# Retention and feed-forward on one core: w1 and w2 loaded by six converting GpSimd transfers, and the order ahead of the fifth step redone

## The chip, the cores and the metric

One Trainium2 chip, one of its cores. The metric is the time of one execution on the device in microseconds (us); the kernel before was run three times, with a median of 176.36 us (176.16 to 177.26). A kernel is compared with the kernel before on the same chip.

## The reference

Four sequences of 768 tokens with 8 heads of 64 go through a retention recurrence, and its output through a feed-forward product. Inputs and output are fp32.

```python
state = gamma[h] * state + outer(k[t], v[t])       # per batch and head
y[t]  = (1 / sqrt(64)) * (q[t] @ state)
x     = y, laid out as 3072 tokens x 512
a, b  = x @ w1, x @ w2                             # 512 -> 1024 each
out   = ((a * b) @ w3) @ w_out                     # 1024 -> 1024 -> 512
```

## The kernel before

The 3072 tokens are cut into 12 steps of 256 (T), three steps for each sequence; "step n" below is one of them. For each step the kernel turns q and k on TensorE (`turn`, L341; the result is copied from PSUM by `turned`), multiplies them into scores (`scores`, L377), masks those on VectorE (`mask`, L397), forms k'v (`kv`, L433), advances the state (`state`), and adds the part from the state (`inter`, L499) to the part from the scores (`av`, L525) in two PSUM banks. `x_out` scales the sum into the fp16 tile `xt`, which is the x of the step. The products x@w1 and x@w2 follow, a multiplied by b gives `ht`, and a product with W3O (L627, L639) gives the rows of the output. W3O is w3 @ w_out, made once at the start: w3 is converted, turned in 128 x 128 blocks, and multiplied with w_out by `w3_mm` (L276), four 256-column matmuls in a call; `w3_out` takes a finished block row out of PSUM.

Steps 0 and 1 use w1 and w2 as they are: `rows(W, n, uh, d)` (L604) is four matmuls of 256 columns with row block d of W (128 of the 512 rows), for half uh of the 1024 columns, and `rows_out` takes each finished bank out, a plain copy for w1 (`pa`) and the multiplication a*b for w2 (`ht`). From step 2 on the products are made with fewer multiplications by sums of weights (`combine`, `sums`, `prod`, L752); that part is a loop from step 3 on and is not touched.

All order is written out by hand: each engine executes its instructions in the order in which the program lists them, and waits where data or a buffer is missing. PSUM is eight banks, each with one name (K, S0, S1, X0, X1, F0, F1, F2) and one buffer; a tile in a bank can be filled only when the last reader of the bank's previous content is done. Names in rows of a trace leave the digit out (psF is F0, F1 or F2).

Inputs come by `fetch`, in the order of the list at the end of the program: every load is 512 KB and is issued on SyncE's queue (SP) into one of 18 fp32 stage tiles `st`. q, k and v come in runs of 512 bytes (128 floats, L85), weights in rows of 4096 bytes (L98, L103). k, q and the weights are then converted to fp16 by a copy on an engine ("s" ScalarE = ACT, "v" VectorE = DVE, "g" GpSimd = POOL; all by line 62), v is multiplied by a decay on POOL (`cast_v`, L65). w1 and w2 are eight such loads between v1 and k2, and 16 conversions: row blocks 0 and 2 in halves of 512 columns (`cast_wc`), blocks 1 and 3 in halves of 64 partitions that change places (`cast_wh`). `fence(n)` is a copy of one column on ACT (L510) that waits for the first half of `inter`.

```python
W1 = [wpool.tile([128, DFF], HP, name=f"w1_{i}") for i in range(4)]
def cast_wh(W, st, d, r, eng):
    copy(eng, W[d][half(1 - r), :], w_st[st, d][half(r), :])
```

Of the kernel before, what the change touches and what calls it, by code (L numbers as in the profile page):

```python
# [21 lines left out]
def kernel(  # L22
# [11 lines left out]
    nc = tc.nc  # L34
# [40 lines left out]
    tok_in = {}  # L75
    source = {"q": q, "k": k, "v": v}

    def load(nm, n, via=None):
        via = via or nc.sync
        b, c = divmod(n, PER)  # L80
        t = new_stage()
# [105 lines left out]
    W1 = [wpool.tile([128, DFF], HP, name=f"w1_{i}") for i in range(4)]  # L187
    W2 = [wpool.tile([128, DFF], HP, name=f"w2_{i}") for i in range(4)]
# [74 lines left out]
    W3_BANK = {4: 'K', 1: 'S0', 2: 'X0', 5: 'F2', 3: 'F0', 6: 'X1', 7: 'F2', 0: 'F2'}  # L263
# [326 lines left out]
    ROW_BANKS = {('a', 0, 0): ('F2', 'X0'), ('a', 0, 1): ('K', 'F1'), ('b', 0, 0): ('S0', 'X0'), ('b', 0, 1): ('X1', 'F1'), ('a', 1, 0): ('S1', 'F0'), ('a', 1, 1): ('K', 'F2'), ('b', 1, 0): ('S1', 'S0'), ('b', 1, 1): ('K', 'F1')}  # L590
# [92 lines left out]
    def cast_w(W, st, d, eng):  # L683
        copy(eng, W[d][:, :], w_st[st, d][:, :])

    def cast_wc(W, st, d, x, eng):
        copy(eng, W[d][:, x * 512 : x * 512 + 512], w_st[st, d][:, x * 512 : x * 512 + 512])

    def cast_wh(W, st, d, r, eng):
        copy(eng, W[d][half(1 - r), :], w_st[st, d][half(r), :])  # L690
# [150 lines left out]
    fetch("k0")  # L841
    fetch("r7")
    fetch("wo3")
# [3 lines left out]
    fetch("r0")  # L847
    fetch("k1")
    fetch("v1")
    fetch("w11")  # L850
    fetch("w10")
    fetch("w13")
    fetch("w12")
    fetch("w21")
    fetch("w22")
    fetch("w20")
    fetch("w23")
    fetch("k2")
# [56 lines left out]
    tables()  # L915
    w3_mm(3, 2)
    w3_mm(4, 1)
    w3_mm(1, 2)
    w3_mm(6, 2)
    w3_mm(3, 1)  # L920
    turn("k", 0, "F1")
    w3_mm(2, 1)
# [4 lines left out]
    w3_mm(3, 3)  # L927
# [4 lines left out]
    w3_mm(2, 3)  # L932
    w3_mm(6, 1)
    w3_mm(3, 0)
    w3_mm(7, 2)
    turned("k", 0, "v")
    w3_out(5, "v")
    turned("q", 0, "v")
    w3_out(1, "v")
    w3_out(4, "s")  # L940
    cast_v(0, "g")
    cast("q", 1, "s")
    scores(0, ("K", "F1"), 0)
    scores(0, ("S0", "S1"), 1)
# [3 lines left out]
    w3_mm(6, 0)  # L948
    w3_mm(7, 3)
# [3 lines left out]
    step_decays()  # L953
    w3_out(3, "v")
    mask(0, 0, 0)
    mask(0, 1, 1)
    mask(0, 1, 0)
    state(0, 1)
    mask(0, 0, 1)
# [3 lines left out]
    turn("q", 1, "F1")  # L963
    turn_w3(0, "S0")
    w3_out(2, "s")
    fence(0)
    state(0, 3)
    turned_w3(0, "v")
    inter(0, 1)
    av(0)  # L970
    cast("k", 1, "s")
    turned("q", 1, "v")
    cast_wh(W1, "w1", 1, 0, "s")
    turn("k", 1, "X0")
    cast_v(1, "g")
    turned("k", 1, "v")
    x_out(0, 0)
    x_out(0, 1)
    w3_mm(0, 2)
    w3_mm(0, 0)  # L980
    scores(1, ("S0", "X0"), 1)
    cast_wh(W1, "w1", 1, 1, "g")
    mask(1, 1, 1)
    w3_mm(0, 1)
# [4 lines left out]
    cast_wc(W1, "w1", 0, 0, "g")  # L989
    cast_wh(W1, "w1", 3, 0, "g")  # L990
    cast_wc(W1, "w1", 2, 1, "g")
    cast_wc(W1, "w1", 2, 0, "g")
    w3_out(0, "s")
    cast_wc(W1, "w1", 0, 1, "s")
    cast_wh(W1, "w1", 3, 1, "s")
    mask(1, 1, 0)
# [3 lines left out]
    rows(W1, 0, 0, 0)  # L1000
    rows(W1, 0, 1, 1)
    inter(1, 0, ("S0", "S1"))
    rows(W1, 0, 1, 3)
    rows(W1, 0, 0, 3)
    rows(W1, 0, 1, 2)
    fence(1)
    mask(1, 0, 0)
    state(1, 2)
    rows_out("a", 0, 1, 0, "s")
    cast_wh(W2, "w2", 1, 0, "v")  # L1010
    cast_wh(W2, "w2", 1, 1, "v")
    cast_wc(W2, "w2", 2, 1, "g")
# [5 lines left out]
    cast_wc(W2, "w2", 2, 0, "s")  # L1018
    cast_wh(W2, "w2", 3, 1, "s")
    x_out(1, 0)  # L1020
    rows(W2, 0, 1, 2)
    rows(W2, 0, 1, 1)
    rows(W2, 0, 0, 1)
    rows_out("a", 0, 0, 0, "v")
    x_out(1, 1)
    state(1, 3)
    cast_wc(W2, "w2", 0, 0, "g")
    cast_wc(W2, "w2", 0, 1, "g")
    cast_wh(W2, "w2", 3, 0, "g")
    combine(3, 0)  # L1030
    combine(1, 1)
    combine(3, 1)
    cast_v(2, "g")
    rows(W2, 0, 0, 0)
    rows(W2, 0, 1, 0)
    rows(W1, 1, 0, 3)
    rows(W1, 1, 0, 0)
    rows(W1, 1, 1, 1)
    rows(W1, 1, 0, 2)
    rows(W2, 0, 0, 2)  # L1040
    rows(W2, 0, 0, 3)
    rows(W1, 1, 0, 1)
    rows(W1, 1, 1, 0)
    rows(W1, 1, 1, 2)
    rows(W1, 1, 1, 3)
    rows(W2, 1, 0, 2)
    rows(W2, 0, 1, 3)
    cast_v(3, "g")
    rows_out("b", 0, 0, 0)
    rows_out("b", 0, 0, 1)  # L1050
    combine(1, 0)
    rows_out("a", 1, 0, 1, "v")
    rows_out("a", 1, 0, 0, "s")
# [214 lines left out]
```

## Time and profile before

| what | value |
|---|---|
| median of the three runs | 176.36 us |
| the profiled execution's own time | 175.95 us |
| its span, first to last instruction | 174.2 us |
| busy: PE, DVE, POOL, ACT | 166.9, 125.6, 91.4, 87.6 us |
| moved by DMA | 39.80 MB |

The profile comes from one execution; the 1.75 us between its span and its time lie outside the instructions. In a timeline row stand the start, the time that the row covers, engine, line, operation, tiles (out<-in), number of matmuls or other instructions, and in brackets the idle time of the engine before it with what ended it. Matmuls overlap, so their pace is the distance between starts, not the printed length, and an idle time of PE is printed only when the previous matmul has quite ended. "PE busy" is therefore no measure of how well it is used.

### The profile page before, as it was taken

To read this page: it belongs to the slowest core of one execution; us is meant where nothing else is said; L and a number is where in the kernel's file an instruction comes from. 1 tells how busy PE (TensorE), PEld (TensorE's weight loads), DVE (VectorE), ACT (ScalarE), POOL (GpSimd) and SP (SyncE) were. 2 spreads that over 40 slices of the span, in tenths; PEclk is the share of its full clock that TensorE was granted. 3 is DMA by queue.
4 is the path that set the end of the run, shared out by engine and by line. 5 is a ranking of instruction groups with operands and counts; after the bars stand their busy time and mean duration, and the time that the engine had idled before them with its cause. 6 is when DMAs were issued, how large, how long until landed. Compare 5 with 4: busy or idle time off the path is not lost.

```text
span 174.2 us, 7306 instructions
## 1 busy us (share of the span) xinstructions
PE 166.9 (96%) x3196; PEld 135.5 (78%) x3196; DVE 125.6 (72%) x250; ACT 87.6 (50%) x159; POOL 91.4 (52%) x105
## 2 busy tenths in 40 slices
PE   7859999999999999999999999999999999999992
PEld 2348977778876699597798977959999598695972
DVE  3253269989989988877878689695896878956370
ACT  3139856545308476281651926618256183571832
POOL 6140465967042916189583792948829366122150
PEclk9999999999999999999999999999999999999999
DMA  5999999999999998999999999999990353091563
GB/s 197 382 416 362 322 312 314 408 403 305 270 249 201 247 213 203 142 237 205 187 213 162 239 217 170 229 216 188 203 180 15 64 217 153 20 399 71 240 245 122
DMA packets 76160, 39.80 MB, mean 228 GB/s; under 512 B 53088, under 2 KB 71776, under 8 KB 76128
## 3 DMA queue, kind: packets, MB, share of 16 engines
q1 hardware_dynamic: 76128, 39.33, 91.6%
q8 instruction: 25, 0.41, 1.1%
q14 instruction: 7, 0.06, 0.1%
HBM read 29.36 MB, written 6.29 MB: 205 GB/s over the span
## 4 chain that ended last, share of the span: by engine, by line
PE 75%; DMA 13%; SPq 7%; DVE 1%; POOL 1%; issue 0%; ACT 0%; POOLq 0%; ACTq 0%
PE psF L752 26%; DMA st<-in_moe_w_dram 13%; PE psF L627 10%; PE psX L627 8%; PE psK L752 5%; PE psX L752 5%; PE psS L627 5%; SPq L85 4%; SPq L98 3%; PE psX L499 2%; PE psF L604 2%; PE psS L604 2%; PE psF L639 2%; PE psX L525 2%; PE psS L386 2%; PE psX L604 1%
## 5 line engine op out<-in xcount | busy, mean ns | idle before, releaser
L752 PEld LDWEIGHTS <-wt 128*128 128x128 f16 x640 | 37.4, 98 | 0.0
L627 PEld LDWEIGHTS <-ht 128*128 128x128 f16 x224 | 20.9, 98 | 14.6
L65 POOL TENSOR_TENSOR c<-u,p 128x512 f32<-128x512 f32 x20 | 25.1, 1276 | 10.5 <-DVE ht L65 8.9
L752 PEld LDWEIGHTS <-w 128*128 128x128 f16 x480 | 28.8, 98 | 1.7
L62 ACT COPY u<-psF 128x512 f32<-128x512 f32 x40 | 23.5, 591 | 7.1 <-PE psF L752 6.9
L65 POOL TENSOR_TENSOR seven<-xt,seven 128x256 f16<-128x256 f16 x9 | 6.0, 670 | 32.7 <-PE psF L752 26.4
L65 POOL TENSOR_TENSOR v<-st,VN 128x1024 f16<-128x1024 f32 x9 | 17.1, 1904 | 5.0 <-PE psK L433 5.0
L752 PE MATMUL psF<-sodd,wt 128*128 128x128 f16 x240 | 18.1, 219 | 0.0
L627 PE MATMUL psF<-w3o,ht 128*128 128x256 f16 (+1 forms) x96 | 17.2, 327 | 0.0
L65 DVE TENSOR_TENSOR c<-psK,u 128x512 f32<-128x512 f32 x10 | 6.9, 692 | 14.1 <-PE psK L752 13.5
L546 DVE TENSOR_TENSOR xt<-psX,YN 128x512 f16<-128x512 f32 x18 | 11.6, 687 | 5.5 <-PE psX L525 5.5
L65 DVE TENSOR_TENSOR ht<-psF,c 128x512 f16<-128x512 f32 x20 | 13.7, 687 | 2.2 <-POOL c L65 1.8
L658 ACT ACTIVATE osb<-psF 128x512 f32<-128x512 f32 x8 | 4.8, 597 | 21.0 <-PE psF L627 21.0
L627 PE MATMUL psX<-w3o,ht 128*128 128x512 f16 (+1 forms) x80 | 15.2, 336 | 0.0
L65 DVE TENSOR_TENSOR ht<-psX,c 128x512 f16<-128x512 f32 x19 | 13.2, 692 | 2.4 <-PE psX L752 0.5
L62 POOL CAST k<-st 128x1024 f16<-128x1024 f32 x9 | 9.4, 1042 | 8.9 <-DMA st<-in_k_dram 8.9
L604 PEld LDWEIGHTS <-w 128*128 128x128 f16 x128 | 12.1, 98 | 2.5 <-POOL w L62 0.6
L276 PEld LDWEIGHTS <-w3t 128*128 128x128 f16 x128 | 11.9, 98 | 1.6
L752 PE MATMUL psX<-xt,w 128*128 128x128 f16 x152 | 11.6, 219 | 0.0
L403 DVE TENSOR_TENSOR am<-psS,keep 128x512 f16<-128x512 f32 x17 | 10.9, 683 | 0.0
L752 PE MATMUL psF<-seven,wt 128*128 128x128 f16 x160 | 10.7, 219 | 0.0
L752 PE MATMUL psF<-xt,w 128*128 128x128 f16 x160 | 10.6, 219 | 0.0
(154 smaller groups left out, 351.5 us busy)
## 6 DMA issues: line engine op xcount, KB each, us to landing
st<-in_moe_w_dram SPq DMA_DIRECT2D x16, 512.0 KB, 8.2
st<-in_q_dram SPq DMA_DIRECT2D x12, 512.0 KB, 6.4
st<-in_k_dram SPq DMA_DIRECT2D x18, 256.0 KB, 4.9
st<-in_v_dram SPq DMA_DIRECT2D x18, 256.0 KB, 5.4
out_dram<-osb SPq DMA_DIRECT2D x9, 512.0 KB, 5.3
st<-in_moe_w_out_dram SPq DMA_DIRECT2D x4, 512.0 KB, 8.3
st<-in_k_dram SPq DMA_DIRECT2D x3, 512.0 KB, 10.8
st<-in_v_dram SPq DMA_DIRECT2D x3, 512.0 KB, 7.9
```

Of the source, the lines that this page charges most:

```text
L62: {"v": nc.vector.tensor_copy, "g": nc.gpsimd.tensor_copy, "s": nc.scalar.copy}[eng](dst, src)
L65: (nc.vector if eng == "v" else nc.gpsimd).tensor_tensor(dst, a, b, op)
L85: via.dma_start(t[:, :].rearrange("p (h x) -> p h x", x=2 * D), src.rearrange("h (p t) d -> p h (t d)", t=2))
L98: nc.sync.dma_start(t[:, :], src[i * 128 : (i + 1) * 128, :])
L276: nc.tensor.matmul(acc[f][:, cols], lhsT=w3t[f][:, g * 128 : (g + 1) * 128], rhs=WO[i][:, r, cols], start=(first and (r, c) == (0, 0)), st ...
L386: nc.tensor.matmul(ps[r][half(g), a, s, :], lhsT=kT[n][half(r), s, a, half(g)], rhs=qchunk(n, r, a, s, g), start=True, stop=True,)
L403: nc.vector.tensor_tensor(t[:, :, :, :].rearrange("p a s i -> p (a s) i"), ps[:, :, :, :].rearrange("p a s i -> p (a s) i"), keep64[:, :]. ...
L546: nc.vector.tensor_tensor(XT[n][:, :, :, :].rearrange("p t a (s x) -> p (a s) t x", s=2)[:, :, :, g * 32 : (g + 1) * 32], x[:, :, :].rearr ...
L604: nc.tensor.matmul(rows_ps[w, n, uh][j // 2][:, j % 2, :], lhsT=W[d][:, f * 128 : (f + 1) * 128], rhs=XT[n][:, :, d, :], start=(first and ...
L627: nc.tensor.matmul(ps[:, x * w : (x + 1) * w], lhsT=HT[n][:, tb, f, :], rhs=W3O[f][:, c0 + x * w : c0 + (x + 1) * w], start=(f == 0 and x ...
L658: nc.scalar.activation(o_tile(n, tb)[:, c0:c1], o_ps.pop((n, tb, c0, c1))[:, :], AF.Copy, scale=final_scale)
L752: nc.tensor.matmul(ps[:, j, :], lhsT=lhsT, rhs=rhs, start=(opens and j == 0 and c == 0), stop=(i in (2, 3, 4) and j == 3 and c == 1), skip ...
```

## The change

The eight loads of w1 and w2, their stage tiles and all 16 conversions are gone. w1 is one fp16 tile of 128 x 4 x 1024, w2 another, and each is filled by three transfers that GpSimd issues and that read fp32 and write fp16: "even" (row blocks 0 and 2, 1 MB read), "upper" and "lower" (the halves of blocks 1 and 3, 512 KB read each, put on the other 64 partitions). `hold` takes the stage tile of k2 early and lets GpSimd write one column of it behind its last transfer, so that the load of k2, and on SP all that stands behind it, waits for that. On SP the loads of r7 (the last rows of w3) and wo3 (the last part of w_out) change places, and so do those of k1 and v1, q2 now comes ahead of k2, and q4 is moved back behind v4. The list that orders all engines up to step 4 is written anew; five entries of the two tables of PSUM banks differ.

```diff
-    W1 = [wpool.tile([128, DFF], HP, name=f"w1_{i}") for i in range(4)]
-    W2 = [wpool.tile([128, DFF], HP, name=f"w2_{i}") for i in range(4)]
+    WA = {nm: wpool.tile([128, 4, DFF], HP, tag=nm, name=nm) for nm in ("w1", "w2")}
+    W1, W2 = ([WA[nm][:, d, :] for d in range(4)] for nm in ("w1", "w2"))
...
-    ROW_BANKS = {('a', 0, 0): ('F2', 'X0'), ('a', 0, 1): ('K', 'F1'), ('b', 0, 0): ('S0', 'X0'), ('b', 0, 1): ('X1', 'F1'), ('a', 1, 0): ('S1', 'F0'), ('a', 1, 1): ('K', 'F2'), ('b', 1, 0): ('S1', 'S0'), ('b', 1, 1): ('K', 'F1')}
+    ROW_BANKS = {('a', 0, 0): ('F2', 'X0'), ('a', 0, 1): ('K', 'F1'), ('b', 0, 0): ('X0', 'S0'), ('b', 0, 1): ('X1', 'F1'), ('a', 1, 0): ('F0', 'S1'), ('a', 1, 1): ('K', 'F2'), ('b', 1, 0): ('F2', 'S0'), ('b', 1, 1): ('K', 'X0')}
...
+    def fetch_w(nm, part):
+        rows_of = {"w1": moe_w1, "w2": moe_w2}[nm].rearrange("(e o r p) n -> o r p e n", o=2, r=2, p=64)
+        if part == "even":
+            src = {"w1": moe_w1, "w2": moe_w2}[nm].rearrange("(e o p) n -> o p e n", o=2, p=128)
+            nc.gpsimd.dma_start(WA[nm][:, 0:4:2, :], src[0])
+        else:
+            r = {"upper": 0, "lower": 1}[part]
+            nc.gpsimd.dma_start(WA[nm][half(1 - r), 1:4:2, :], rows_of[1, r])
+    def hold(nm, n):
+        gate[nm, n] = t = new_stage()
+        nc.gpsimd.memset(t[:, 0:1], 0.0)
...
-    cast("q", 1, "s")
+    fetch_w("w1", "upper")
+    fetch_w("w1", "lower")
...
     inter(0, 0, ("F0", "X1"))
-    turn("q", 1, "F1")
     turn_w3(0, "S0")
     fence(0)
+    cast("q", 1, "s")
...
     inter(0, 1)
+    turn("q", 1, "F0")
     av(0)
-    cast("k", 1, "s")
+    cast("k", 1, "v")
     turned("q", 1, "v")
...
+    hold("k", 2)
+    fetch("q2")
+    fetch("k2")
...
-    mask(1, 1, 0)
     mask(1, 0, 1)
     state(1, 1)
...
+    mask(1, 1, 0)
     state(1, 2)
...
-    rows(W2, 0, 1, 2)
     rows(W2, 0, 1, 1)
     rows(W2, 0, 0, 1)
...
     rows(W1, 1, 1, 2)
     rows(W2, 1, 0, 2)
...
     half_h(2, 0, 0)
+    prod(2, 1, 7)
     prod(2, 1, 3)
     prod(2, 0, 7)
-    prod(2, 1, 7)
```

What the new list does on three engines, in the stretch between the scores of step 0 and those of step 1. First VectorE, before, from the state of step 0 (t1, s32) over the turned w3 block 0 (w3t), q1 (qT) and k1 (kT) to x of step 0 (xt) and the first two masks of step 1 (am_717, am_792):

```order
L62 CAST t1_594<-psF0_530 128x256
L397 TENSOR_TENSOR am_596<-psS0_504,keep_82 128x512
L62 CAST w3o_7_114<-psF2_470 128x512
L65 TENSOR_TENSOR s32_599<-psK_531,t1_594 128x256
L62 COPY w3t_630<-psS0_616 128x1024
L62 COPY qT_670<-psF1_607 128x1024
L62 COPY kT_684<-psX0_673 128x1024
L541 TENSOR_TENSOR xt_686<-psF0_601,YS_88 128x4x2x64
L541 TENSOR_TENSOR xt_686<-psX1_602,YS_88 128x4x2x64
L397 TENSOR_TENSOR am_717<-psX0_699,keep_82 128x512
L397 TENSOR_TENSOR am_792<-psK_728,keep_82 128x512
```

And now:

```order
L62 CAST t1_558<-psF0_509 128x256
L62 CAST w3o_7_108<-psF2_440 128x512
L65 TENSOR_TENSOR s32_561<-psK_510,t1_558 128x256
L62 COPY w3t_589<-psS0_569 128x1024
L397 TENSOR_TENSOR am_591<-psS1_458,keep_82 128x512
L62 CAST k16_638<-st_143 128x8x2x64
L62 COPY qT_640<-psF0_597 128x1024
L62 COPY kT_651<-psX0_642 128x1024
L541 TENSOR_TENSOR xt_668<-psF0_563,YS_88 128x4x2x64
```

k1's conversion (k16_638, from the load's stage tile) now stands on VectorE ahead of the copy of the turned q1, and the turned q1 lies in bank F0 (psF0_597), which is also the bank of the first half of step 0's x (psF0_563). Five rows on, the mask of bank K follows a mask and the state instead of one mask:

```order
L397 TENSOR_TENSOR am_702<-psX0_685,keep_82 128x512
L397 TENSOR_TENSOR am_767<-psS0_684,keep_82 128x512
L65 TENSOR_TENSOR t1_769<-psS1_726,t0_584 128x256
L397 TENSOR_TENSOR am_809<-psK_709,keep_82 128x512
L65 TENSOR_TENSOR s32_811<-psX1_727,t1_769 128x256
```

Second ScalarE, before, where w3o are finished rows of W3O and q16_484 and k16_668 the converted q1 and k1:

```order
L62 CAST w3o_4_111<-psK_319 128x512
L62 CAST q16_484<-st_143 128x8x2x64
L62 CAST w3o_6_113<-psX1_397 128x512
L62 CAST w3o_2_109<-psX0_338 128x512
L510 COPY fence_626<-psX1_602 64x1
L62 CAST k16_668<-st_147 128x8x2x64
L62 CAST w1_1_96<-st_151 64x1024
```

And now:

```order
L62 CAST w3o_4_105<-psK_289 128x512
L62 CAST w3o_2_103<-psX0_312 128x512
L62 CAST w3o_6_107<-psX1_384 128x512
L510 COPY fence_578<-psX1_564 64x1
L62 CAST q16_580<-st_137 128x8x2x64
L62 CAST w3o_0_101<-psF1_671 128x512
```

q1's conversion has moved behind the fence of step 0, and no conversion of w1 follows.

Third GpSimd, before, where v16_482 and v16_682 are v0 and v1 with their decay, w3h the converted w3 block 0, GS a constant, t0 the state handed to step 1:

```order
L65 TENSOR_TENSOR v16_482<-st_141,VS_86 128x8x2x64
L62 CAST w3h_577<-st_145 128x1024
L210 MEMSET GS_90 64x64 x8
L65 TENSOR_TENSOR t0_628<-s32_599,GS_90 128x256
L65 TENSOR_TENSOR v16_682<-st_149,VS_86 128x8x2x64
L62 CAST w1_1_96<-st_151 64x1024
L62 CAST w1_0_95<-st_153 128x512
```

And now:

```order
L65 TENSOR_TENSOR v16_452<-st_135,VS_86 128x8x2x64
L691 DMA w1_95<-in_moe_w1_dram 64x2x1024 x2
L62 CAST w3h_548<-st_139 128x1024
L688 DMA w1_95<-in_moe_w1_dram 128x2x1024
L691 DMA w2_96<-in_moe_w2_dram 64x2x1024 x2
L65 TENSOR_TENSOR t0_584<-s32_561,GS_90 128x256
L65 TENSOR_TENSOR v16_586<-st_141,VS_86 128x8x2x64
L688 DMA w2_96<-in_moe_w2_dram 128x2x1024
L695 MEMSET st_653 128x1
```

Five transfers now stand between v0 and v1, and the sixth and the write that frees k2's load behind v1.

More of the change, by code (lines that the diff above doesn't have):

```diff
@@ L952 @@
     cast_w3(0, "g")
-    step_decays()
+    fetch_w("w1", "even")
     w3_out(3, "v")
+    mask(0, 1, 0)
     mask(0, 0, 0)
-    mask(0, 1, 1)
-    mask(0, 1, 0)
+    mask(0, 0, 1)
     state(0, 1)
-    mask(0, 0, 1)
     w3_out(7, "v")
@@ L1066 @@
     rows(W2, 1, 1, 1)
+    turn("q", 2, "S0")
     o_part(0, 1, 0, "F0")
-    turn("q", 2, "S0")
-    turn("k", 2, "F2")
+    turn("k", 2, "K")
     turned("k", 2, "s")
@@ L1100 @@
     av(2)
-    o_copy(1, 0)
     turned("k", 3, "v")
-    state(3, 1)
-    cast("q", 3, "g")
     turn("q", 3, "S1")
@@ L1111 @@
     fetch("v5")
+    fetch("q6")
     fetch("k6")
-    fetch("q6")
+    cast("k", 4, "g")
     cast_v(4, "g")
-    cast("k", 4, "g")
     x_out(2, 0)
+    state(3, 1)
+    x_out(2, 1)
+    sums(2, 3)
+    sums(2, 1)
     state(3, 2)
-    x_out(2, 1)
+    sums(2, 2)
     state(3, 3)
-    sums(2, 1)
-    sums(2, 3)
-    sums(2, 2)
     state(3, 4)
     turned("q", 3, "s")
-    cast("q", 4, "v")
+    o_copy(1, 0)
     sums(2, 4, "v")
+    prod(2, 1, 1, "F0")
     scores(3, ("S1", "X1"))
@@ L1146 @@
     keep_part(2, 1, "u2")
-    turn("k", 4, "X1")
+    turn("k", 4, "S1")
+    turned("k", 4, "v")
     half_h(2, 0, 0)
-    turned("k", 4, "v")
+    prod(2, 1, 7)
     prod(2, 1, 3)
     prod(2, 0, 7)
-    prod(2, 1, 7)
     prod(2, 1, 2)
```

181 lines of the change are left out of this document (78 added, 103 removed).

## The prediction

> **What bounds the kernel now.** I read the page first, its busy shares and the 40 slices.
>
> ```profile
> span 174.2 us, 7306 instructions
> PE 166.9 (96%) x3196; PEld 135.5 (78%) x3196; DVE 125.6 (72%) x250; ACT 87.6 (50%) x159; POOL 91.4 (52%) x105
> ...
> PEclk9999999999999999999999999999999999999999
> DMA  5999999999999998999999999999990353091563
> ```
>
> PE is busy to the end at the full granted clock, and the 16 DMA engines are full for the first three quarters. Next, the windows of the stretch that the change rewrites (columns: busy time and count of PE, PEld, DVE, ACT, POOL, then clock, DMA share, GB/s).
>
> ```profile
> 12.00:26.00 14.00, 13.78 (x174) 12.06 (x176) 6.25 (x9) 10.68 (x20) 5.49 (x5) 1.00 1.08 338
> 26.00:34.00 8.00, 8.00 (x201) 6.33 (x193) 7.54 (x13) 4.24 (x7) 5.79 (x12) 1.00 1.06 355
> 34.00:42.00 8.00, 7.78 (x139) 5.93 (x128) 7.10 (x14) 4.38 (x8) 5.71 (x9) 1.00 1.06 374
> 42.00:50.00 8.00, 8.00 (x76) 7.17 (x75) 7.45 (x11) 2.15 (x4) 2.36 (x2) 1.00 1.12 257
> ```
>
> From 12 to 50 us PE misses 0.44 us of 38. VectorE is at 7.1 to 7.5 of 8, so it has little room of its own, and DMA is full (shares over 1 are transfers that overlap on an engine). Third, PE's timeline at the places where the order changes; the last row is from the chain of work that ended last.
>
> ```profile
> 18.12 0.60 PE L276 MATMUL psK<-wo,w3t 128*128 128x256 f16 x4
> 18.56 0.60 PE L276 MATMUL psS<-wo,w3t 128*128 128x256 f16 x4
> ...
> 23.33 0.62 PE L341 MATMUL psF<-ident,q 128*128 128x128 f16 x8 [0.22 <-POOL q L62]
> ...
> 27.18 0.21 PE L433 MATMUL psF<-v,k 64*64 64x64 f16 x1
> ...
> 28.97 0.30 PE L499 MATMUL psX<-qT,t 64*64 64x128 f16 x4
> ...
> 30.21 0.25 PE L525 MATMUL psF<-am,v 64*64 64x128 f16 x2
> ...
> 30.88 0.62 PE L341 MATMUL psX<-ident,k 128*128 128x128 f16 x8
> ...
> 34.89 0.39 PE L604 MATMUL psK<-xt,w 128*128 128x256 f16 x2
> ...
> 38.87 0.92 PE L604 MATMUL psX<-xt,w 128*128 128x256 f16 x4
> ```
>
> ```profile
> 39.42 0.37 PE psX L604 x2
> ```
>
> A call of four matmuls takes 0.44 us (18.12 to 18.56), and starts follow each other at that pace nearly everywhere. What can still be won are two waits: 0.22 us at q0's turn, and about 0.3 at 39.4 (the four from 38.87 on last 0.92, where four at full pace last 0.60). All else is PE's own work, and the change leaves the number of its matmuls alone. So the gain is capped near 0.5 us, and the question is what new waits come in, since whatever PE waits goes to the end.
>
> **The conversions taken away.** From the view of the stage tiles:
>
> ```profile
> L62 POOL CAST w<-st x9: 609/614/1275, 32.9 to 41.5; 128x512 f16<-128x512 f32 x6, 64x1024 f16<-64x1024 f32 x3
> ...
> L62 ACT CAST w<-st x5: 619/1043/1043, 32.3 to 41.5; 64x1024 f16<-64x1024 f32 x3, 128x512 f16<-128x512 f32 x2
> ...
> L62 DVE CAST w<-st x2: 686/686/687, 37.4 to 38.1; 64x1024 f16<-64x1024 f32 x2
> ```
>
> About 7, 4.4 and 1.4 us of engine time go, all beside PE's work but for the two on DVE: they hold up a copy out of PSUM for which PE waits at 39.4. That wait goes: -0.3.
>
> **The new order, by engines.** These rows carry the rest (DVE, ACT, POOL):
>
> ```profile
> 27.89 0.42 DVE L62 CAST t<-psF 128x256 f16<-128x256 f32 x1
> 28.22 0.68 DVE L397 TENSOR_TENSOR am<-psS,keep 128x512 f16<-128x512 f32 x1
> ...
> 30.91 0.68 DVE L62 COPY qT<-psF 128x1024 f16<-128x1024 f16 x1
> 31.53 0.69 DVE L62 COPY kT<-psX 128x1024 f16<-128x1024 f16 x1
> ...
> 33.34 0.68 DVE L397 TENSOR_TENSOR am<-psX,keep 128x512 f16<-128x512 f32 x1
> 34.10 0.69 DVE L397 TENSOR_TENSOR am<-psK,keep 128x512 f16<-128x512 f32 x1
> ```
>
> ```profile
> 29.31 0.15 ACT L510 COPY fence<-psX 64x1 f32<-64x1 f32 x1
> ...
> 32.32 1.04 ACT L62 CAST w<-st 64x1024 f16<-64x1024 f32 x1 [1.79 <-DMA st<-in_moe_w_dram]
> ...
> 39.29 0.59 ACT L62 COPY pa<-psX 128x512 f32<-128x512 f32 x1 [0.80 <-PE psX L604]
> ```
>
> ```profile
> 22.23 1.04 POOL L62 CAST q<-st 128x1024 f16<-128x1024 f32 x1 [2.04 <-DMA st<-in_q_dram]
> 24.05 1.93 POOL L65 TENSOR_TENSOR v<-st,VS 128x1024 f16<-128x1024 f32 x1 [0.77 <-DMA st<-in_v_dram]
> 26.99 1.04 POOL L62 CAST w3h<-st 128x1024 f16<-128x1024 f32 x1 [1.01 <-DMA st<-in_moe_w_dram]
> ...
> 30.25 0.73 POOL L65 TENSOR_TENSOR t<-s,GS 128x256 f16<-128x256 f32 x1 [0.85 <-DVE s L65]
> ...
> 34.96 1.03 POOL L62 CAST w<-st 64x1024 f16<-64x1024 f32 x1 [0.32 <-DMA st<-in_moe_w_dram]
> 36.24 1.17 POOL L62 CAST w<-st 128x512 f16<-128x512 f32 x2 [0.24 <-DMA st<-in_moe_w_dram]
> ```
>
> First, up to av of step 0. q0's turn stays where its load puts it (23.33), but 18 products stand before it now, not 19: all behind it is 0.44 later. kv of step 0 stood behind two products after the scores and now stands behind four, another 0.87: 27.18 + 1.31 = 28.5. It takes 0.4, so VectorE's t starts at about 28.9. Between it and the copy of the turned q1 stand t (0.33, the distance 27.89 to 28.22) and five more instructions, w3o, s, w3t, a mask and the conversion of k1, at 0.6 each (as 30.91 to 31.53): the copy runs from 32.2 to 32.9. av writes bank F0, out of which that copy reads, so it starts at 32.95 and not at 30.21. q1's conversion behind the fence (29.31 + 0.44, 0.15, then some 1.05 and the turn) gives q1 at 31.6 and hides behind VectorE. That is +2.7.
>
> Second, bank K for the first products with w1. From av to k1's turn PE takes 0.67 (30.21 to 30.88), k1's copy comes 0.65 later: 34.27. The mask that empties K started 2.57 after that copy; a mask and the state (0.6 and 0.33) now stand ahead of it, less the 0.16 by which it came late there (33.34 to 34.10 instead of 0.6): 37.6, over at 38.3. PE gets there at 32.95 + 4.68 (30.21 to 34.89) = 37.6 and waits to 38.35. Late by 3.45 in all.
>
> Third, three banks that are refilled too soon. The last product into a bank at 38.98 (the second of the pair at 38.87) had its copy done at 39.29 + 0.59 = 39.88: 0.9 after that issue, when the next matmul could go after 0.11. In the new order bank F2 is refilled by the very next call (w1's last products of step 1, then w2's first): +0.8. X0 (w2 of step 0) and the first bank of step 2 (product 7 behind product 6) have one call of 0.44 between: +0.4 each. No engine's freed time shortens these; they are PE, ScalarE and PE in turn.
>
> The order alone then costs 3.45 - 0.3 + 0.8 + 0.4 + 0.4 = 4.75 us. Nothing gives it back: behind 50 us PE has no wait of that size to fill.
>
> **The transfers.** Their issue on POOL and their pace are not in this trace. For the issue I take 1.03, POOL's own time for the same 64x1024 (bounds: 0.4, which is what most SP issues last, and 1.93, its longest instruction here). Five of them, the w3 conversion, the state and v1 end at 25.98 + 5.15 + 1.04 + 0.73 + 1.93 = 34.8; kv of step 1 needs v1 near 37, so up to 1.45 each is hidden, and at 1.93 it would cost 2.4. SP's issues, and the first conversion that waits for one:
>
> ```profile
> 0.81 1.35 SPq L98 DMA_DIRECT2D st<-in_moe_w_dram  x3
> ```
>
> ```profile
> 4.30 0.62 ACT L62 CAST w3h<-st 128x512 f16<-128x512 f32 x1 [2.21 <-DMA st<-in_moe_w_dram]
> ```
>
> The pace: weights land every 1.28 us (34.96 to 36.24 are two such). r0 lands at 26.99 and the first w at 32.32, with k1 and v1 between, so those take some 1.7 each, and since they change places k1 would land at 30.4, 1.2 before VectorE wants it (31.6). The first transfer is issued at 25.98, its data move from about 28 on (an estimate: one issue of 1.03, and half of the 2.2 us by which the first load of all, issued at 0.81 and there at 4.30, took longer than its 1.28), when v1 and k1 still need 2.4 us. Bounds for what it adds: nothing, if k1 is served first, and 6.4, if all five transfers (3 MB, 7.7 us) go ahead of it, less that 1.2. I take equal turns, as between two queues that are both full: k1 at 32.8, +1.2. The sixth transfer is issued behind v1, at 34.8, and competes with k2 and what follows: by the same turns it lands near 45.4, and the product that reads it first is due at 44.5: +0.9. Sum of the transfers +2.1.
>
> [...]
>
> **Sum.** 175.95 + 4.75 + 2.1 = 182.8 us, against the profiled execution's own 175.95; the median, 176.36, is 0.4 above that.
>
> **The rivals.**
> k1 starved. Loads of k take 1024 runs in 1.7 us, 27 ns of an engine for each, weights 128 rows in 1.28, 160 ns. If an engine takes one run of each queue in turn, SP gets a seventh while w1 and w2 move. k1 lands at 37 to 39, VectorE and with it av wait as long: +5.4 to 8 instead of +1.2, in all about 188. For it: DMA is full and w's rows are eight times as long. Against: between transfers POOL converts w3, which may let k1 through.
> Transfers that cost nothing. If k1 lands before 31.6 and the sixth before 44.5, the order's 4.75 remain: 180.7. For it: a transfer that writes half the bytes may be quicker.
> Slow conversion. If a converted 512 KB takes 2.56 us and not 1.28, the eight take 20 us from 28 on, and w2 is complete no sooner than 48 instead of 44.5, later with SP's share; +4 to +10 on the order's cost, about 189.
> Not slower. VectorE is not what binds: if the copy of the turned q1 is done by 30.6, when PE is there, the first term shrinks to 0.44 and bank K is free in time. Then 0.44 - 0.3 + 1.6 remain, 177.7. It is decided by av's start, at or below 31; against it stands VectorE's 7.54 of 8 us.
>
> **How the numbers follow.** Forecast 0.37, k1 starved 0.20, transfers free 0.24, slow conversion 0.12, not slower 0.07. The likeliest alone reaches from 181.5 to 184.5 by the issue and the turns. The range 180.2 to 190 leaves out the not slower case and the ends of the two slow ones, about 0.17. A gain of over 1% (1.76 us, about what a measurement of this kernel can tell from no change) is barred by the cap of 0.5 us: 0.01. Within 1%: 0.05. Slower: 0.94.
>
> **What would show it.** After: av of step 0 (PE L525) at 33 or later, behind a VectorE copy into qT that follows a conversion k<-st ended by a DMA; PE waiting for DVE am at bank K, and 0.8 us ahead of the products of w2 in F2; six DMA issues on POOL of about 1 us between v0 and v1; PE's windows from 28 to 52 no longer full. An av at 31, or k1's conversion without a wait, would prove me wrong; PE waiting on the w tiles themselves would speak for slow conversion.

## The result and the profile after

The changed kernel takes 186.64 us (median of 4 runs, 184.92 to 186.81), the kernel before 176.49 beside it: 1.054 times as long, with a 95% interval of 1.048 to 1.059. The forecast was 182.8 with a range of 180.2 to 190. The profiled execution took 186.79 us, its span 185.0: 10.8 more than before. Ratios here and below leave out runs over 1.5% above the fastest of the same kernel, and the kernel before has such runs too: on one chip four of eight took 180.6 to 182.1 us, at mean clocks of 0.979 to 0.990.

First the page of the changed kernel: the span, PE's share, and of the 40 slices PE and the granted clock.

```profile
span 185.0 us, 7267 instructions
...
PE 170.8 (92%) x3196; PEld 137.3 (74%) x3196; DVE 127.6 (69%) x247; ACT 82.7 (45%) x155; POOL 89.8 (49%) x103
...
PE   7979697598978989999999999999999999999993
...
PEclk9999999669999999999999999999999999999999
```

PE has the same 3196 matmuls, with holes between slices 5 and 15; and two digits of the clock are 6, which no slice before was. The windows of the changed kernel (the same stretches as before, and one more; the column behind POOL's is the clock):

```profile
26.00:34.00 8.00, 5.13 (x109) 3.88 (x109) 6.71 (x11) 1.78 (x3) 7.58 (x10) 0.97 1.14 245
34.00:42.00 8.00, 7.21 (x124) 4.98 (x123) 4.30 (x8) 0.59 (x1) 0.04 (x1) 0.61 1.12 220
42.00:50.00 8.00, 7.37 (x104) 6.05 (x105) 4.96 (x9) 1.82 (x4) 0.00 (x0) 1.00 0.95 243
50.00:58.00 8.00, 6.32 (x57) 5.37 (x56) 5.73 (x8) 2.96 (x4) 5.92 (x4) 1.00 1.22 235
```

PE loses 2.9 us from 26 to 34. From 34 to 42 it looks busy, but at a granted clock of 0.61: busy time says nothing of the pace. PE's waits by what ended them, in the changed kernel from 20 to 80 us (the kernel before has one row there, 0.2 us at q0's turn):

```profile
PE psF L525 <- DVE qT L62: 2.7, 1, 2.7
PE psS L256 <- POOL w3h L62: 1.6, 1, 1.6
PE psS L604 <- DVE ht L65: 1.0, 1, 1.0
PE psK L604 <- DVE am L397: 0.8, 1, 0.8
PE psF L604 <- ACT pa L62: 0.7, 1, 0.7
PE psF L341 <- ACT q L62: 0.5, 1, 0.5
PE psX L499 <- DVE am L397: 0.5, 1, 0.5
PE psX L604 <- ACT pa L62: 0.2, 1, 0.2
PE psF L757 <- ACT u L62: 0.2, 1, 0.2
```

The row on top is av of step 0. Rows 4, 5, 8 and 9 are the banks K, F2, X0 and the first bank of step 2, as the prediction named them. No row has a DMA of w: PE never waits for the weights.

av waits for the copy of the turned q1. VectorE and GpSimd there, after the change:

```profile
31.02 0.68 DVE L397 TENSOR_TENSOR am<-psS,keep 128x512 f16<-128x512 f32 x1
32.21 1.54 DVE L62 CAST k<-st 128x1024 f16<-128x1024 f32 x1 [0.52 <-DMA st<-in_k_dram]
33.67 0.68 DVE L62 COPY qT<-psF 128x1024 f16<-128x1024 f16 x1
```

```profile
25.87 1.38 POOL L691 DMA_DIRECT2D w<-in_moe_w_dram  x2
27.50 1.04 POOL L62 CAST w3h<-st 128x1024 f16<-128x1024 f32 x1 [0.24 <-DMA st<-in_moe_w_dram]
28.48 0.73 POOL L688 DMA_DIRECT2D w<-in_moe_w_dram  x1
29.20 1.21 POOL L691 DMA_DIRECT2D w<-in_moe_w_dram  x2
30.59 0.72 POOL L65 TENSOR_TENSOR t<-s,GS 128x256 f16<-128x256 f32 x1 [0.18 <-DVE s L65]
31.28 1.92 POOL L65 TENSOR_TENSOR v<-st,VS 128x1024 f16<-128x1024 f32 x1
33.15 0.78 POOL L688 DMA_DIRECT2D w<-in_moe_w_dram  x1
```

VectorE is ready at 31.7, waits for k1 (landed at 32.19), and then its conversion takes 1.54 us, not the 0.6 by which such instructions follow each other. It ends at 33.75, 0.55 us behind GpSimd's multiplication of v1 (31.28 + 1.92 = 33.20). The six issues take 0.6 to 0.8 us each.

Where the 10.7 us went, by starts on PE (before, after, and what the change added up to that point):

| place | before | after | added | the prediction's sum |
|---|---|---|---|---|
| q0's turn | 23.33 | 23.30 | 0.0 | 0.0 |
| av of step 0 | 30.21 | 34.40 | 4.2 | 2.7 + 1.2 |
| first product of w1 in bank K | 34.89 | 42.39 | 7.5 | 3.45 + 1.2 |
| end of the last matmul | 171.18 | 181.89 | 10.7 | 4.75 + 2.1 |

Up to av the sum holds within 0.3 us. It falls short by 2.6 us between av and bank K, and by 1.0 behind it.

### The profile page after: what moved, and what is told of

Read it like the earlier page. It is cut to its first block, busy times and chain, and to the rows that moved or that the text cites. A ratio compares the mean times of both kernels' runs of the same rounds, so it can differ in the third digit from the quotient of the medians.

```text
span 185.0 us, 7267 instructions
## 1 busy us (share of the span) xinstructions
PE 170.8 (92%) x3196; PEld 137.3 (74%) x3196; DVE 127.6 (69%) x247; ACT 82.7 (45%) x155; POOL 89.8 (49%) x103
## 4 chain that ended last, share of the span: by engine, by line
PE 72%; SPq 9%; DMA 8%; DVE 8%; issue 1%; ACT 1%; DVEq 0%
PE psF L757 24%; PE psF L627 8%; PE psX L627 7%; DMA st<-in_k_dram 5%; PE psK L757 5%; SPq L85 5%; PE psX L757 5%; PE psS L627 4%; DVE wt L65 3%; DMA st<-in_moe_w_dram 3%; SPq L103 2%; PE psX L499 2%; PE psF L604 2%; PE psF L276 2%; PE psX L525 2%; DVE ht L65 2%
## 5 line engine op out<-in xcount | busy, mean ns | idle before, releaser
L65 POOL TENSOR_TENSOR v<-st,VN 128x1024 f16<-128x1024 f32 x9 | 17.6, 1952 | 0.0
L62 POOL CAST q<-st 128x1024 f16<-128x1024 f32 x8 | 8.3, 1037 | 18.1 <-DMA st<-in_q_dram 18.1
L604 PEld LDWEIGHTS <-w 128*128 128x128 f16 x128 | 12.2, 98 | 5.0 <-issue 3.5
L276 PEld LDWEIGHTS <-w3t 128*128 128x128 f16 x128 | 12.7, 103 | 2.6 <-issue 0.6
L757 PE MATMUL psF<-xt,w 128*128 128x128 f16 x160 | 10.7, 219 | 0.0
```

Of the source, the lines that this page charges most:

```text
L62: {"v": nc.vector.tensor_copy, "g": nc.gpsimd.tensor_copy, "s": nc.scalar.copy}[eng](dst, src)
L65: (nc.vector if eng == "v" else nc.gpsimd).tensor_tensor(dst, a, b, op)
L276: nc.tensor.matmul(acc[f][:, cols], lhsT=w3t[f][:, g * 128 : (g + 1) * 128], rhs=WO[i][:, r, cols], start=(first and (r, c) == (0, 0)), st ...
L604: nc.tensor.matmul(rows_ps[w, n, uh][j // 2][:, j % 2, :], lhsT=W[d][:, f * 128 : (f + 1) * 128], rhs=XT[n][:, :, d, :], start=(first and ...
L757: nc.tensor.matmul(ps[:, j, :], lhsT=lhsT, rhs=rhs, start=(opens and j == 0 and c == 0), stop=(i in (2, 3, 4) and j == 3 and c == 1), skip ...
```

## The experiments

The theory after reading the trace: the order and k1 make av late, as forecast; in addition the long wait lowers PE's granted clock (0.61 on average from 34 to 42 us), and a PE that runs late shifts VectorE's work on w1 and w2 under GpSimd's multiplications of v, where a combination takes 2.07 us instead of 0.69. The rivals: the transfers' traffic is the loss; or the new order's further waits (w3 block 7, the banks) are.

**The wait filled.** All else is the changed kernel.

```
     turn("q", 1, "F0")
+    warm(12, "F2")
     av(0)
```

> Twelve matmuls of zeros, 0.21 us each and read by nobody, are put ahead of av of step 0, where PE waits 2.9 us; the rest is the changed kernel. Theory (PE's idleness at 31.7 to 34.4 makes the clock drop): the granted clock stays at 1.00 between 34 and 42 us, the products of w3 block 0 go at 0.109 us each instead of 0.213, and the time falls by 1.5 to 2.3 us, to about 184.6, with av still at 34.4. Rival, that these matmuls are slow because of the transfers or of their operands: they stay at 0.213 and the time stays at 186.6 or grows.

182.20 us (182.07 to 182.38), 1.032 times the time before (1.027 to 1.037). Against the changed kernel's 186.64 some 4.4 came off, more than the 1.5 to 2.3 expected. PE's waits in this kernel from 20 to 80 us:

```profile
PE psK L604 <- DVE am L397: 0.8, 1, 0.8
PE psF L604 <- ACT pa L62: 0.7, 1, 0.7
PE psS L256 <- POOL w3h L62: 0.7, 1, 0.7
PE psF L341 <- ACT q L62: 0.5, 1, 0.5
PE psX L604 <- ACT pa L62: 0.2, 1, 0.2
PE psF L757 <- ACT u L62: 0.2, 1, 0.2
PE psF L341 <- POOL q L62: 0.2, 1, 0.2
```

av starts at 34.38 as in the changed kernel, and bank K's product at 39.77 instead of 42.39: 2.6 us, without a single instruction less. The two waits for DVE ht (L604) and for DVE am (L499), which lengthen the distance from start to start by 1.12 and 0.72 us in the changed kernel, are gone as well.

**The changed kernel again**, since a low clock could be a matter of one chip.

> The changed kernel itself, unaltered, beside the others on one chip. Theory (its last 4.4 us over the kernel with matmuls in the wait come from the granted clock, which falls after PE idled 2.7 us): mean clock near 0.98, 24 matmuls or so between 35.4 and 40.4 at half pace, about 186.6 us. Rival, that the low clock belonged to one chip: clock 1.00 and about 183.

185.88 us (184.12 to 187.12), 1.054 times before (1.047 to 1.061). Its four runs had mean clocks of 0.982, 0.982, 0.991 and 0.990 and took 186.7, 187.1, 185.0 and 184.1 us. On the same chip the kernel before ran at 0.99 to 1.00 in eight runs, so the low clock goes with the changed kernel, and it comes in portions. The windows are laid where this trace's granted clock changes, at 33.15 and 39.98:

```profile
29.74:33.15 3.41, 1.44 (x22) 1.11 (x21) 3.41 (x5) 1.20 (x2) 2.85 (x3) 1.00 1.15 227
33.15:36.57 3.42, 2.12 (x42) 1.89 (x42) 1.29 (x3) 0.00 (x0) 0.94 (x3) 0.50 1.13 213
36.57:39.98 3.41, 3.41 (x31) 2.15 (x30) 2.15 (x4) 0.00 (x0) 0.00 (x0) 0.50 1.12 216
39.98:43.39 3.41, 2.63 (x66) 1.99 (x65) 2.93 (x6) 0.59 (x1) 0.00 (x0) 1.00 1.12 285
```

Half clock for 6.83 us, two times 3.41, behind a stretch of 3.41 in which PE was busy for 1.44. In the first trace of the changed kernel it is the same: half from 33.45 to 40.27, behind 1.10 us of work in 3.42. In both traces the first half-clock stretch has 2.12 or 2.46 us of work and is followed by another; behind the second, with 3.41, the clock is whole again. The two stretches go with this trace's mean clock of 0.982; one goes with 0.991 in the profiled run with twelve pieces, below. From these it is the author's estimate that the runs at 0.990 and 0.991 had one, which costs up to half of 3.41; they are some 2 us shorter.

PE was not idle throughout the stretch ahead: 1.44 us of work in it did not keep the clock up. The kernel before has a stretch near that at its start, 6.63 to 10.05 with 1.74 us of work and a full clock behind it; whether its runs at a lower mean clock come from there no trace shows.

**A wait alone, in the kernel before.** VectorE copies the turned w3 block 0 five times more; w1 and w2 come as they did.

```
+    slow = w3p[0]
     turned_w3(0, "v")
+    for _ in range(5):
+        copy("v", w3t[0][:, :], slow[:, :])
```

> The kernel before, with w1 and w2 through stage tiles, in which VectorE copies the turned w3 block 0 six times instead of once (0.6 us each, 3.0 us more), so that PE waits about 2.6 us at 31.3 us, where it waited for nothing. If a wait costs only itself: 176.3 + 3.0 = 179.3 us and the clock at 1.00. If idleness of that length lowers the granted clock by itself (theory): a stretch of half-pace matmuls behind it, mean clock 0.98 to 0.99, and 181 to 182 us.

185.03 us (183.90 to 185.63), 1.054 times before (1.050 to 1.058): neither number. In the profiled run (183.90 us) the clock stayed at 1.00 though PE waited 3.2 us in one piece; in the other three it was 0.97 to 0.98 (the kernel before, on the same chip: 0.99 to 1.00). The windows of the profiled run, counted in steps of 3.41 from its first change of clock (5.95 us):

```profile
29.85:33.26 3.41, 1.70 (x53) 1.33 (x50) 3.07 (x5) 1.78 (x2) 2.90 (x3) 1.00 1.02 405
33.26:36.67 3.41, 1.79 (x28) 1.32 (x29) 3.38 (x6) 0.00 (x0) 3.22 (x5) 1.00 1.03 413
```

The wait fell across an edge of these steps, and neither window has less than 1.70 us of work. From this the author's estimate is that it matters where a wait lies against the steps; the three runs at a lower clock have no trace to show it. A longer wait alone did not explain this run, which is 4.6 us over the 179.3: PE's waits of 1.2 us for DVE ht (L604) and 2.2 for DVE am (L499) come back here, in a kernel that has neither the new order nor the transfers. VectorE's combinations of w1 and w2, and GpSimd, in this run:

```profile
49.15 2.44 DVE L65 TENSOR_TENSOR wt<-w,w 128x1024 f16<-128x1024 f16 x1
...
58.08 4.67 DVE L65 TENSOR_TENSOR wt<-w,wt 128x1024 f16<-128x1024 f16 x3
```

```profile
49.11 1.94 POOL L65 TENSOR_TENSOR v<-st,VS 128x1024 f16<-128x1024 f32 x1 [4.85 <-DMA st<-in_v_dram]
...
58.42 2.34 POOL L65 TENSOR_TENSOR v<-st,VN 128x1024 f16<-128x1024 f32 x1
```

In the kernel before, the first takes 0.69 us (at 45.49) and the three 2.02 (from 52.65), between two multiplications of v (48.47 to 50.40, 55.41 to 57.32). Here the first begins 0.04 us behind GpSimd's and ends at 51.59, 0.54 behind its end. VectorE was late by 3.7 us (49.15 instead of 45.49), and its own work then met GpSimd's, which starts when v lands.

**One combination moved under GpSimd.** The filled-wait kernel with one line put three instructions later.

```
-    combine(1, 0)
     rows_out("a", 1, 0, 0, "v")
     rows_out("b", 0, 0, 1)
     rows_out("a", 1, 0, 1, "v")
+    combine(1, 0)
```

> The changed kernel with the twelve matmuls in the wait, in which one combination of w1 and w2 on VectorE (128x1024, both inputs in SBUF) is put three instructions later, from 50.25 to about 52.05 us, behind the start of GpSimd's multiplication of v2 (51.90 to 53.83 in that run). Nothing is added. Theory (such a combination, 0.69 us by itself, stands still while GpSimd's instruction goes on): it takes 2.0 to 2.5 us, the copies behind it are late by 1.3 to 1.8, PE waits 0.9 to 1.3 us for them at the products with w2 of step 1, as the changed kernel's trace shows at 56.19, and the time is 183.1 to 183.6 instead of 182.2 us. Rival, that the late VectorE of the changed kernel comes from its later products alone: the combination takes 0.69 us wherever it stands, and the time stays at 182.2.

182.62 us (182.46 to 182.88), 1.036 times before (1.032 to 1.041). VectorE and GpSimd:

```profile
52.36 1.29 DVE L65 TENSOR_TENSOR wt<-w,w 128x1024 f16<-128x1024 f16 x1
53.58 0.67 DVE L65 TENSOR_TENSOR ht<-pa,psF 128x512 f16<-128x512 f32 x1
```

```profile
52.08 1.04 POOL L62 CAST q<-st 128x1024 f16<-128x1024 f32 x1 [17.74 <-DMA st<-in_q_dram]
53.08 2.37 POOL L65 TENSOR_TENSOR v<-st,VS 128x1024 f16<-128x1024 f32 x1
```

q3 had landed later than in the other run, so the combination met q3's conversion. The mechanism is shown: 1.29 us instead of 0.69, ended 0.53 us behind GpSimd's instruction (53.12), and then GpSimd's next took 2.37 instead of 1.93. The expected size was missed: VectorE had 0.6 us of slack behind it and PE did not wait, so the 182.6 proves no cost. That the 1.12 us at 56.19 in the changed kernel are this mechanism rests on its trace, not on a run of its own:

```profile
52.87 2.07 DVE L65 TENSOR_TENSOR wt<-w,w 128x1024 f16<-128x1024 f16 x1
```

```profile
51.46 1.04 POOL L62 CAST q<-st 128x1024 f16<-128x1024 f32 x1 [17.43 <-DMA st<-in_q_dram]
52.47 1.93 POOL L65 TENSOR_TENSOR v<-st,VS 128x1024 f16<-128x1024 f32 x1
```

The combination begins behind the start of GpSimd's v2 and ends at 54.94, 0.54 behind its end. In the filled-wait kernel it stands at 50.25 to 50.94, just ahead of q3's conversion (50.90), and takes 0.69. So VectorE moved by 2.6 us with PE, and GpSimd by 0.6 with q3's landing. The new list also put GpSimd's conversion of q3 ahead of its multiplication of v2; in the kernel before, v2 comes first. The 0.72 us at L499 follow in the same way from the four combinations at 61.31, which take 4.45 us (2.73 in the filled-wait kernel) beside GpSimd's v3 from 61.26 on.

**k1 first.** The forecast's second cause of a late av, taken away.

```
-    fetch("v1")
     fetch("k1")
+    fetch("v1")
```

> Only the place of two loads changes: k1 is asked for ahead of v1 again. Theory (the copy of the turned q1 waits behind k1's conversion, and that for k1's landing at 32.19, and the 2.9 us wait of PE that follows also lowers the granted clock for about 5 us): k1 lands near 29.5 to 30, VectorE converts it without a wait from 31.6 on, av starts at about 32.9 instead of 34.40 (1.45 us), and the slowed stretch shrinks or goes (up to 2.3 us: 12 matmuls later by 0.104 each, k1's turn 0.4, the scores 0.5). Forecast 183 to 185.2 us. Rival, that the converting transfers hold back any load of SP's whatever its place: av stays near 34.4 and the time at 186.6.

182.43 us (181.28 to 187.38, 6 runs), 1.033 times before (1.023 to 1.043). The median lies below the 183 to 185.2 expected. k1 lands at 29.0, VectorE converts it in 0.68 us, and av starts at 33.02:

```profile
31.68 0.68 DVE L62 CAST k<-st 128x1024 f16<-128x1024 f32 x1
32.28 0.68 DVE L62 COPY qT<-psF 128x1024 f16<-128x1024 f16 x1
```

That is the 32.95 that the prediction gave for the order alone. Bank K's product, at 38.43, now waits 0.9 us for the DMA of w (landed at 38.38), where without transfers it waits 0.8 for the mask, to 38.27: with av this early, mask and weights come at the same time. The profiled run has a clock of 0.999; four others, at 0.98 to 0.99, reach 187.4 us. That the waits of 0.7 us (q1's turn) and 1.4 us (av), close together, lower the clock there is the author's estimate and not shown, since those runs have no trace. GpSimd multiplied v1 from 32.26 to 34.19 here, beside the copy of the turned q1, which reads PSUM and took 0.68 us all the same; the VectorE instructions that took longer beside GpSimd in the traces above (1.54, 2.44, 1.29 and 2.07 us) go from SBUF to SBUF.

**No transfers.** GpSimd fills the tiles of w1 and w2 with a constant; nothing of w1 and w2 is read.

```
-            nc.gpsimd.dma_start(WA[nm][:, 0:4:2, :], src[0])
+            nc.gpsimd.memset(WA[nm][:, 0:4:2, :].bitcast(FP), 5.3912e-19)
```

> The six transfers are left out: GpSimd fills the same parts of the w1 and w2 tiles with a constant in their place, so nothing of w1 and w2 is read from memory. The order of all else is that of the changed kernel. Theory (most of the loss is the order's): k1 lands by 30.4, av starts near 32.9, the waits at w3 block 7's turn (1.8 us), at bank K (0.9), X0 (0.4), F2 (0.9) and in step 2 (0.4) stay; 186.6 - 1.45 - 2.3 = 182.9, and up to 0.7 less where a late k2 or q2 was waited for: 181.5 to 183.5. Rival, that the transfers by their traffic are the loss: the time comes down to 178 or less.

182.67 us (182.27 to 183.31), 1.035 times before (1.028 to 1.042), so the traffic of the transfers is not what the new order pays for; what it adds in the changed kernel is the late k1, and with it a longer wait ahead of av: 2.7 us instead of 1.3. av starts at 32.97 and bank K's product at 38.27, where the prediction's sum for the order alone has 32.95 and 38.35. The total is above its 180.7, and the rows say why: without transfers q3, which GpSimd converts ahead of v2, lands earlier (47.32 instead of 51.31), GpSimd multiplies v2 from 48.44 to 50.37, and VectorE's combination of 48.76 takes 2.15 us; PE loses 1.20 us to DVE ht and 0.53 at L499.

**The transfers alone.** The order, banks and first loads (up to v1) of before, with the six transfers at the same places of GpSimd's list; the loads of q2 and behind come as in the changed kernel.

```
     cast_v(0, "g")
+    fetch_w("w1", "upper")
+    fetch_w("w1", "lower")
...
     cast_w3(0, "g")
+    fetch_w("w1", "even")
...
-    cast_wh(W1, "w1", 1, 0, "s")
```

> The kernel before with its own order, banks and loads, in which only the eight loads of w and their conversions are replaced by the six converting transfers, issued at the same places of GpSimd's list as in the changed kernel (the loads of k2 and behind wait for a write of GpSimd behind v1, as there). Theory (the order is most of the loss): av near 30.2, no wait over 0.5 us up to 44, then perhaps 0.9 at the first products with w2, whose sixth transfer lands at 43.7: 176 to 178 us. Rival, that the transfers are the loss: k1 and v1 come late and it takes 182 or more.

181.53 us (180.97 to 182.63), 1.029 times before (1.021 to 1.037): not the 176 to 178 expected, nor the rival's 182 or more. PE's waits from 20 to 80 us:

```profile
PE psK L604 <- DMA w<-in_moe_w_dram: 2.5, 1, 2.5
PE psF L341 <- POOL q L62: 1.5, 1, 1.5
PE psX L604 <- DMA w<-in_moe_w_dram: 1.3, 1, 1.3
PE psX L499 <- DVE am L397: 1.0, 1, 1.0
```

With av at its old place PE does wait for the weights: blocks 0 and 2 of w1, the second and the fourth that the products read, come in one transfer and land at 37.68; the last of w2 lands at 43.37. (The 1.5 us at q0's turn are no loss: PE came there that much earlier, and the turn stands at 23.27.) Each half of the change costs some 5 to 6 us by itself. With the wait filled the whole change costs 5.9, so at full clock the two don't add: the new order comes to the weights late enough for them. Unfilled, it costs 10.2, and the rest is the clock and what follows from it.

**The transfers in twelve pieces.** Block by block in the order of use, q2's load held back too, and the eight fills of GS moved ahead of q0's conversion.

```
+        if d % 2 == 0:
+            nc.gpsimd.dma_start(WA[nm][:, d, :], src[d * 128 : (d + 1) * 128, :])
+        else:
+            for r in range(2):
+                nc.gpsimd.dma_start(WA[nm][half(1 - r), d, :], src[d * 128 + r * 64 : d * 128 + r * 64 + 64, :])
...
+    hold("q", 2)
```

> The order of the kernel before with converting transfers, now twelve instead of six (each block of 128 rows by itself, in the order in which the products read the blocks), q2's load held back as k2's is, and the eight fills of GS ahead of q0's conversion. Theory (the converting transfers are not slow by themselves: what PE waited for, 2.5 us at the first products with w1 and 1.3 us at those with w2, was that two blocks of one transfer land together and late, and that q2 took turns with them): both waits fall below 0.5 us and the time to 177 to 178.5 us. Rival, that the conversion slows the stream: w2 is still complete no sooner than 43 us, and the time stays at 180 to 181.5.

180.93 us (180.39 to 181.57), 1.030 times before (1.027 to 1.033). The waits for w fell to 0.5 and 0.6 us, nearly as the theory had it (below 0.5), and the time stayed as its rival had it. What was won there was lost behind: three combinations take 4.43 us from 54.42 on, over GpSimd's v3 (54.57 to 56.86), and PE waits 1.9 us for DVE am at L499 (1.0 with the six transfers). After that wait this trace has one half-clock stretch, 62.60 to 66.02; in the 3.41 us ahead of it PE was busy for 1.51.

**The banks.** With k1 first, the bank table, the mask of bank K and product 7 of step 2 as before the change.

```
+    mask(1, 1, 0)
     mask(1, 0, 1)
     state(1, 1)
...
-    mask(1, 1, 0)
     state(1, 2)
...
-    prod(2, 1, 7)
     prod(2, 1, 3)
     prod(2, 0, 7)
+    prod(2, 1, 7)
```

> The changed kernel with k1 asked for ahead of v1, and with the bank table, the place of the mask that empties K, and the place of product 7 of step 2 put back as they were before the change (two banks of step 0's and step 2's tiles follow the table). Theory (four waits of PE of 1.04, 0.41, 0.89 and 0.39 us come from these lines alone): 2.7 us less than with k1 first alone, from 182.3 to about 179.6 us. Rival, that VectorE is late anyway and the waits move to the next place: no more than 1 us gained, 181.3 or above.

Its four runs took 180.94 to 185.64 us, the first at a mean clock of 1.00 and the others at 0.98; there is no interval. In the profiled first run the four waits, taken from start to start (1.04, 0.40, 0.89, 0.39 us in the run with k1 first) are down to 0.16, 0.18, 0.0 and 0.43, and 0.25 and 0.33 are new at two other banks. From av to the end it takes 141.8 us instead of 143.4: 1.6 of the 2.7 that the theory gave. Of this, the 0.9 at bank K is not the mask's alone: with k1 first the DMA of w ended that wait, and it is gone here because this trace is also 1.2 us later at av (34.22 instead of 33.02), while the weights land at 38.60 instead of 38.38.

**w3 block 7.** In the filled-wait kernel r7 goes ahead of wo3 again (two lines change places).

> The changed kernel with the twelve matmuls in the wait ahead of av of step 0, as in the run above, and with r7 loaded ahead of wo3 again. Theory (all behind q0's turn hangs on q0's landing at 22.1 us, so the 0.9 to 1.8 us that PE waits at the turn of w3 block 7 are only spent there instead of two calls later): that wait goes, the one at q0's turn grows to about 1.2 us, q0's turn stays at 23.3 and the time at 182.2 us. Rival, that the wait for r7 is a loss of its own: 0.8 to 1.4 us less, 181 us.

182.28 us (182.18 to 183.30), 1.036 times before (1.031 to 1.042): as the theory had it. Measured from start to start, the turn of block 7 waits 0.4 instead of 0.9 us, q0's turn stands at 23.26, and the time is the same. The second row of the changed kernel's waits, 1.6 us, cost nothing.

**All repairs at once.**

```
+    fetch("r7")
     fetch("wo3")
-    fetch("r7")
...
     turn("q", 1, "F0")
+    warm(6, "F2")
     av(0)
```

> The changed kernel with all repairs at once: k1 ahead of v1, r7 ahead of wo3, the bank table, the mask and product 7 as before the change, and six matmuls of zeros in what is left of the wait ahead of av. What stays of the change: the six transfers, k1's conversion on VectorE ahead of the copy of the turned q1, q1's conversion behind the fence. Theory (the waits add up, 1.4 us at av and 0.7 at q1's turn stay): 181.3 (k1 first, at full clock) less the 1.6 us that the banks gave from av on, 179.0 to 180.0 us with no run above 181, since the clock stays at 1.00; no version with these transfers and this order reaches 176.3. Rival, that the repairs free VectorE and GpSimd from each other as well: 178 us or less.

180.08 us (179.86 to 181.02), 1.024 times before (1.017 to 1.030), at clocks of 1.00, just above the 179.0 to 180.0 expected. That is the best version with the six transfers and this order of q1 and k1, and slower than the kernel before. It still waits 0.8 us at bank K, now for the DMA of w (38.29), so putting the mask back gains nothing there while the transfer lands at 38.25.

## Why the prediction was right in sign and short in size

- **av of step 0** (+2.7 by the order, +1.2 by k1): measured 4.2. k1 first alone gave back 1.38 of it (34.40 to 33.02). The sum is right, its second part by two errors that cancel: k1 landed at 32.19, not 32.8, and its conversion took 1.54 us, not 0.6.
- **Bank K** (late by 3.45, with k1 4.65): 4.88 in the filled-wait kernel (34.89 to 39.77), where the clock stays up. Right.
- **Banks F2, X0 and step 2** (0.8, 0.4, 0.4): 0.89, 0.40, 0.39, each behind ScalarE's copy as forecast, and without the 0.3 at 39.4. Right as waits; how much of them the old banks give back is not cleanly shown (see the run on the banks).
- **The issues** (1.03 each, hidden): 0.60 to 0.78, hidden.
- **The sixth transfer** (+0.9): nothing. It landed at 43.67, and the products that read it came later than that. With k1 first, where all is earlier, PE loses 0.4 us to it (landed at 44.69).
- **Equal turns** (k1 at 32.8, 2.4 us late): k1 landed at 32.19. Without transfers it lands at 30.46 (30.4 in the prediction), so they made it 1.7 us late. (The rows named for the 1.7 us of k1 and v1, 26.99 and 32.32, leave 2.0 for each; the figure still holds, since k1 took 1.8 and v1 1.65 before the change.) The view of the issues, for k1, q2 and the first transfer (last column: us from issue to landing):

```profile
st<-in_k_dram SPq DMA_DIRECT2D x1, 512.0 KB, 9.8
```

```profile
st<-in_q_dram SPq DMA_DIRECT2D x1, 512.0 KB, 19.7
```

```profile
w<-in_moe_w_dram POOLq DMA_DIRECT2D x1, 256.0 KB, 7.3
```

GpSimd's queue, first used at 25.87, carries its first packet at 28.1, as estimated; k1 then takes 4.1 us for what takes 2.4 without transfers. So its delay is near that of equal turns, but the turns are not equal: from 29 to 31 us GpSimd's queue has 81 to 84% of the engines' time and SP's 28 to 36%, and from 31 to 32.2 they have 46 and 66%. Behind k1 it is worse: from 34 to 38 us 102.5 and 9.8%. q2, next in SP's queue, was issued at 24.19 and lands at 43.90, 11.7 us behind k1, for some 1.7 us of data. SP's share from 34 to 38 us is even less than the seventh of the "k1 starved" rival, but from 38 to 43.7 it is 53%, so one ratio does not describe it. Nothing needed q2 by then.
- **Slow conversion**: refuted. With the old order v1, q2 and w1 and w2 land from 28.70 to 43.37; less an estimated 1.75 each for v1 and q2 (by the 1.65 and 1.8 above), the eight 512 KB take some 1.40 us each, and before the change 1.39 (30.30 to 41.43).
- **"Nothing gives it back: behind 50 us PE has no wait of that size to fill"** and, ahead of it, the sum as a list of waits. This is the step that failed, in two places. A wait was priced at its own length: behind the 2.7 us ahead of av the clock was 0.50 for 6.83 us, +2.6 us up to bank K. And the work behind 50 us was taken to move as a whole: GpSimd's work there starts on landings (q3's, ahead of v2) and moved by 0.6 us, VectorE's combinations moved by 2.6, onto it, and PE lost 1.12 and 0.72 us more.

By terms: 6.85 forecast, +0.3 at av, +0.1 at the banks, -0.9 for the sixth transfer, +2.6 clock, +1.8 collisions: 10.7, as measured. The filled-wait kernel, which has neither of the last two, takes 182.2 us against the forecast's 182.8.

What stays open: how little work in a window lowers the clock (1.51 us of 3.41 did, 1.70 did not); what lowers it in the runs that have no trace, those of the kernel before among them; by what rule the two queues share the engines; and whether pieces issued still earlier could make the transfers free with the old order, whose best median here is 180.9.

## What to carry to other kernels

A wait on the engine that bounds a kernel can cost more than its length: here a granted clock of 0.50 followed one of 2.7 us for 6.83 us, and one of 1.9 us, in the run with twelve pieces, for 3.41. So look at the granted clock behind each such wait, and try matmuls that nobody reads in those that can't be removed (here they took off 4.4 us). Delays need not shift a schedule as a whole: here GpSimd's work that starts on q3's landing moved by 0.6 us while VectorE's moved by 2.6 and came to lie on top of it. Try both halves of a change alone before adding their costs; here each cost 5 to 6 us, and the two together 6 at full clock (182.2 against 176.3).

## What the runs showed of the hardware

- In the three traces with a lower clock it was 0.50 for one or two stretches of 3.41 us and 1.00 ahead of and behind them. At full clock, it was halved behind 1.10, 1.44 and 1.51 us of PE work in such a step (the changed kernel, the same again, twelve pieces), and not behind 1.70 and 1.79 (a wait alone) and 1.74 (the kernel before); at half clock, 2.12 and 2.46 us did not bring it back, 3.41 did.
- In five cases a VectorE instruction of 128x1024 from SBUF to SBUF that started while GpSimd ran a two-input or converting instruction took 1.29 to 2.44 us, where others take 0.69, and ended 0.53 to 0.55 us behind it (33.75, 33.73, 54.94, 51.59 and 53.65 us against GpSimd's ends at 33.20, 33.18, 54.40, 51.05 and 53.12). A copy out of PSUM took 0.68 us beside such an instruction (at 32.28 with k1 first, beside a multiplication from 32.26 to 34.19).
- The six transfers, which convert f32 to f16, read 512 KB in some 1.40 us among full queues with the old order (with the estimate above), where the loads before the change took 1.39, and in the changed kernel each took GpSimd 0.6 to 0.8 us to issue.
